# Linear attention and a residual MLP on one core: the beta2 product, the token mix, k^T v and VectorE's share rearranged, with a planner that looks ahead

## The chip, the cores and the metric

The kernel runs on one core of a Trainium2 chip. The metric is the device time in microseconds of one execution. TensorE (PE) multiplies matrices, VectorE (DVE), ScalarE (ACT) and GpSimd (POOL) do the elementwise work, SyncE (SP) issues most of the transfers.

## The reference

Eight batches, 8 heads of 64, 576 tokens; x has 512 features per token.

```python
kv  = einsum('bhsd,bhse->bhde', k, v)
out = einsum('bhsd,bhde->bhse', q, kv)
x   = out / sqrt(mean(out*out, -1) + 1e-6) * g_norm      # then heads side by side: [8, 576, 512]
a1  = alpha1 * x + beta1
u   = x + lam * einsum('ts,bsd->btd', w_tok, a1)
a2  = alpha2 * u + beta2
y   = u + lam * (maximum(a2 @ w_ch1, 0) @ w_ch2)         # w_ch1 512x2048, w_ch2 2048x512
```

## The kernel before

The whole problem is one program without loops on the device: Python calls `P.op(engine, cost, function, reads, writes)` for each group of instructions, and a planner (`Prog.plan`, `Prog.schedule`) orders them. It holds a cost for each op, makes a list schedule with them over all engines and the 8 banks of PSUM, works back from due times (`mark`) to new priorities for 8 rounds, keeps the best, shakes its priorities at random with a seed, and writes the last schedule down as each engine's fixed order. An engine takes the first op of its queue that is ready at the planned moment. On the chip each engine then follows its own list and waits on semaphores where an op needs another engine or a transfer. Before the first product of batch 0's first channel stage, whenever TensorE would have nothing ready in the plan, the planner puts in a product on zeros (`warm`, L1429).

A batch b goes through these stages:

- k, v and q are loaded in f32 (`load_kv`, `load_q`). Rows 0 to 511 of each head go to 128 partitions, 4 rows each, and the last 64 rows, the tail, to tensors of their own (kft, vft, qft). Batch 0 is loaded instead in two halves of four heads as 64 partitions by 9 rows (`load_first`, `nine`).
- `kv_groups`: k^T v per head in f32; two main groups (L691, 128 rows by 64 columns of the array) and one tail group (L701, 64x64). ScalarE and VectorE split the result into two bf16 parts and copy it to the other half of the partitions (L718, L723, L726). Batch 0 uses 64x64 quadrants (`kv_first`, L628).
- q is split in two bf16 parts (`split_q`, L582) and transposed: by TensorE for batch 1 (L605), by DMA for later batches; batch 0 is transposed in f32 (L649).
- `qkv_groups`: q times kv in pairs of token chunks (L782 with L401 on the held weights, tail L863; batch 0 L789), squares on ScalarE (L819), sums on VectorE (L821), square root on ScalarE, reciprocal, the normalised x (L840), then rt = x * (alpha1*lam*g) in bf16 on VectorE (L844; tail rtt, L892) and x*g in place on GpSimd (L848; tail L895).
- `tok_groups`: the token mix. W_tok^T lies in wt: slots 0 to 3 hold 128 rows each, slots 4 and 5 both hold the last 64 rows, at partitions 0 to 63 for even batches and 64 to 127 for odd ones, and each one also holds a row of W_tok's sums against a row beta1*lam in rtt; the rest is zeros. Each of four token chunks takes 5 passes of 512 columns (L920), and the tails of two batches are mixed together after the odd one (L942). Batch 0 has its own order in two halves of the features (`tok_first`, L972). VectorE adds the result to x (L927).
- u is scaled by alpha2 (L933) and transposed to a2t by DMA (L1037). Batches 0 and 1 are transposed by TensorE in four blocks of 128 features (L1007), and alpha2 and beta2 come in with the evacuation (L1017).
- `ch1_groups`: 16 groups of 4 products. Even batches take 512 tokens (L1056), odd ones 640 as 2 x 320 with the tails of both batches (L1075). relu goes to ht (L1046, L1045). From batch 2 on, beta2's part is a bias hb, which batch 0 gets from a one-column product behind each of its 64 products, on the weights already in the array (L401 out of b2c).
- `ch2_groups`: 16 products per token chunk (L1121), added to u by VectorE (L1131) and written out. w_ch2 is scaled by lam as it is cast to bf16 (L1357).

The q.kv groups of batch b+1 are given among the first-stage groups of batch b, the token mix behind them, and k^T v of batch b+2 among the second-stage groups. SP's queue is first in, first out: transfers that are given in a chain keep their order, and a transfer that waits holds those behind it. The order of all other ops is the planner's.

Of the kernel before, what the change touches and what calls it, by code (L numbers as in the profile page):

```python
# [15 lines left out]
NH = 8  # L16
S = 576
# [32 lines left out]
class Prog:  # L50
# [6 lines left out]
    def __init__(self, nc, stack):  # L57
# [9 lines left out]
        self.spare = 0.0  # L67

# [54 lines left out]
    def plan(self, due, rounds, seeds):  # L123
# [40 lines left out]
        def shake(pri, seed):  # L164
            rnd = random.Random(seed)
            return {o: pri[o] + (rnd.gauss(0.0, 2.0) if rnd.random() < 0.1 else 0.0)
                    for o in movable}
# [12 lines left out]
    def schedule(self):  # L180
# [67 lines left out]

        while left:
            progressed = False  # L250
            for e, q in queues.items():
                while q and free[e] <= t + 1e-9:
# [3 lines left out]
                    for o in cands:  # L256
                        if not ready(o, t):
                            continue
                        if takes_port(o, e) and port_free > t + 1e-9:
                            continue  # L260
                        if isinstance(o.eng, tuple) and better_elsewhere(o, e, t):
                            continue
                        pick = o
                        break
# [142 lines left out]
def bass_transnormer_attn__then__resmlp_affine_kernel(  # L407
# [15 lines left out]
    with ExitStack() as stack:  # L423
# [14 lines left out]
        b2c = sb("b2c", [128, 4], BF16)  # L438
        hb = sb("hb", [128, 16], F32)
        eps = sb("eps", [128, 1], F32)  # L440
        kf = sb("kf", [128, 2, NH, 4, DH], F32)
        vf = sb("vf", [128, 2, NH, 4, DH], F32)
        qf = sb("qf", [128, NH, 4, DH], F32)
        kft = sb("kft", [128, 2, 4, DH], F32)
        vft = sb("vft", [128, 2, 4, DH], F32)
# [18 lines left out]
        a2t = sb("a2t", [128, 4, TP], BF16)  # L464
# [9 lines left out]
        def nine(tile, a):  # L474
            return tile[:, a].rearrange("p h c d -> p (h c d)")[:, 0:1152].rearrange(
                "p (x c d) -> p x c d", x=2, c=9)

# [38 lines left out]

        HALVES = (slice(0, 4), slice(4, 8))
        ALL = (slice(0, 8),)

        def load_first(a):  # L520
            for key, src, tile in (("kf", k, kf), ("vf", v, vf)):
                P.op("SP", 0.6, lambda e, src=src, tile=tile: e.dma_start(
                    nine(tile, a).rearrange("p x c d -> p x (c d)"),
# [11 lines left out]
        def load_kv(b, go=()):  # L535
            j = (b + 1) % 2
            for tile, tl, src, n in ((kf, kft, k, "kf"), (vf, vft, v, "vf")):
                P.op("SP", 0.6, lambda e, tile=tile, src=src: e.dma_start(
                    tile[:, j].rearrange("p h c d -> p h (c d)"),
                    src[b, :, 0:512, :].rearrange("h (p c) d -> p h (c d)", c=4)),  # L540
                    r=go, w=[(n, j)], dma_us=3.4)
                for g in range(2):
                    P.op("SP", 0.5, lambda e, tl=tl, src=src, g=g: e.dma_start(
                        tl[64 * g:64 * g + 64, j],
                        src[b, 4 * g:4 * g + 4, 512:576, :].rearrange("h s d -> s h d")),
                        w=[(n + "t", j, g)], dma_us=0.4)
# [71 lines left out]

        def kv_first():

            def group(a):
                t = P.ptile(2)

                def f(e):
                    for c in range(9):
                        for x, y in ((0, 0), (0, 1), (1, 0), (1, 1)):
                            r = slice(64 * y, 64 * y + 64)
                            m = e.matmul(t.ap(slice(64 * x, 64 * x + 64))[:, y, 0:64],  # L628
                                         nine(kf, a)[r, x, c, :], nine(vf, a)[r, x, c, :],
                                         start=(c == 0), stop=(c == 8), skip_group_check=True)  # L630
                    return m
                P.op("PE", 1.22, f, r=[("kf", a), ("vf", a)], w=[t])
# [43 lines left out]

        def kv_groups(b):
            buf = (b + 1) % 2
# [6 lines left out]
            def main(a):  # L685
                ts.append(P.ptile(1))

                def f(e):
                    for c in range(4):
                        for h in range(4 * a, 4 * a + 4):  # L690
                            m = e.matmul(out(h), kf[:, buf, h, c, :], vf[:, buf, h, c, :],  # L691
# [5 lines left out]
            def tails():  # L697
                def f(e):
                    for h in (0, 4, 1, 5, 2, 6, 3, 7):
                        rows = slice(64 * (h // 4), 64 * (h // 4) + 64)  # L700
                        m = e.matmul(out(h), kft[rows, buf, h % 4, :], vft[rows, buf, h % 4, :],  # L701
                                     start=False, stop=True, skip_group_check=True)
                    return m
                P.op("PE", 0.4, f, r=[(n + "ft", buf, g) for n in "kv" for g in range(2)], w=ts)
# [40 lines left out]
        def rv(b, cs, lo=0, hi=DM):  # L745
            rows = rows_of(b, cs[0])
            if cs[0] == 4:
                return rtt[rows, b % 2, lo:hi]
# [14 lines left out]
        def qkv_groups(b):  # L763

            def group(cs, hs):
# [30 lines left out]
                if b == 0:  # L796
                    P.op("PE", 0.28 * nc_, f32, r=QT + KVD + [("kv32", h0 // 4, i)
# [37 lines left out]
                else:  # L835
# [7 lines left out]
                P.op(dve_pool(64 * m) if b == 0 else "DVE", dve_sb(64 * m),  # L843
                     lambda e: e.tensor_tensor(out=r_, in0=x, in1=eb, op=ALU.mult),  # L844
                     r=xk + ["e1"], w=[kk for c in cs for kk in rkeys(b, c, hs)], pri=-100, port=True)
                for i, c in enumerate(cs):
                    xc = x3[:, i] if nc_ > 1 else x3
                    P.op("POOL", pool_us(64 * nh), lambda e, xc=xc: e.tensor_tensor(  # L848
                        out=xc, in0=xc, in1=g_bc[rows, None, :].to_broadcast([nr, nh, DH]),
                        op=ALU.mult), r=xkeys(b, c, hs) + ["g"], w=xkeys(b, c, hs), pri=-50)  # L850
            def tail():
# [30 lines left out]
                for a in range(2):  # L882
# [9 lines left out]
                P.op("DVE", dve_sb(512), lambda e: e.tensor_tensor(  # L892
                    out=rv(b, (4,)), in0=x, in1=e1g_bc[rows, :], op=ALU.mult),
                    r=xk + ["e1"], w=rkeys(b, 4), pri=-100, port=True)
                P.op("POOL", pool_us(512), lambda e: e.tensor_tensor(  # L895
# [6 lines left out]
        def tok_w(b, sc, c):  # L902
            ws = sc if sc < 4 else 4 + b % 2
            return wt[:, ws, 128 * c:min(128 * c + 128, S)]
# [4 lines left out]
        def wtk(sc, b=0):  # L909
            return [("wtm", sc)] if sc < 4 else [("wts", 4 + b % 2, lo) for lo in (0, 512)]  # L910

        def tok_groups(b):
            def group(cs):
                n = len(cs)
                t = P.ptile(n)
                rows = rows_of(b, cs[0])
                for i, c in enumerate(cs):
# [544 lines left out]
```

## Time and profile before

| | us |
|---|---|
| median of 3 runs (lowest, highest) | 368.38 (367.87, 368.93) |
| the profiled execution | 368.05 |
| its span, first to last instruction | 366.2 |
| TensorE busy | 360.6 |
| VectorE busy | 198.4 |
| ScalarE busy | 159.2 |
| GpSimd busy | 81.7 |

The granted TensorE clock was 1.0 throughout. A busy TensorE counts each product from its start to the end of its result, 0.38 us for 512 columns, while the next starts 0.216 us after it; so costs on TensorE are read from starts, or from the chain, whose pieces follow each other without overlap. A row of the chain has its start, its length and its engine and line; a row of the timeline has start, length, engine, line, operation, output and inputs; a group of instructions has count, busy time, mean in ns, and the idle time before it with who ended it.

### The profile page before, as it was taken

What the parts mean: (1) busy time and instruction counts of PE and PEld (TensorE: products, weight loads), DVE (VectorE), ACT (ScalarE), POOL (GpSimd) and SP (SyncE); (2) the same over time, 40 slices, a digit from 0 to 9 for tenths busy, and PEclk for the clock granted to TensorE, in tenths of its full rate; (3) what the DMA queues carried; (4) which work ended last, traced back from release to release, by engine and by line L of the source; (5) the groups of instructions that cost most, each with busy time, mean ns of one, the idle gap of its engine ahead of it and who ended that gap; (6) DMA issues with size and microseconds to landing.
All of it is one profiled execution on the core that took longest, in us unless ns stands there. A gap on an engine that the chain in (4) does not pass through costs nothing.

```text
span 366.2 us, 7069 instructions
## 1 busy us (share of the span) xinstructions
PE 360.6 (98%) x3164; PEld 205.8 (56%) x2876; DVE 198.4 (54%) x313; ACT 159.2 (43%) x268; POOL 81.7 (22%) x71
## 2 busy tenths in 40 slices
PE   7999999999999999999999999999999999999996
PEld 3787445467754554457654554457654554457644
DVE  4287699773973197735764176915933165720021
ACT  2464974237830298107650188107630186007600
POOL 4064602700450007100530006400620006200000
PEclk9999999999999999999999999999999999999999
DMA  8999999999777897439904499233404110420012
GB/s 257 319 290 319 384 382 273 265 250 249 211 141 158 246 259 178 101 94 309 230 18 115 138 304 177 50 110 85 90 7 108 59 30 0 59 100 30 0 57 88
DMA packets 92423, 59.87 MB, mean 163 GB/s; under 512 B 59549, under 2 KB 82341, under 8 KB 92264
## 3 DMA queue, kind: packets, MB, share of 16 engines
q1 hardware_dynamic: 92368, 59.41, 62.5%
q8 instruction: 24, 0.39, 0.5%
q14 instruction: 7, 0.06, 0.0%
q10 hardware_dynamic: 24, 0.01, 0.0%
HBM read 38.56 MB, written 9.44 MB: 131 GB/s over the span
## 4 chain that ended last, share of the span: by engine, by line
PE 97%; DMA 2%; SPq 0%; DVE 0%; issue 0%
PE ps L1121 34%; PE ps L1075 19%; PE ps L1056 16%; PE ps L920 8%; PE ps L691 4%; DMA qf<-in_q_dram 2%; PE ps L401 2%; PE ps L782 2%; PE ps L789 1%; PE ps L942 1%; PE ps L972 1%; PE ps L1007 1%; PE ps L1429 1%; PE ps L649 1%; PE ps L1102 1%; PE ps L701 1%
## 5 line engine op out<-in xcount | busy, mean ns | idle before, releaser
L1121 PE MATMUL ps<-w,ht 128*128 128x512 bf16 x560 | 126.0, 379 | 0.0
L848 POOL TENSOR_TENSOR xm<-xm,g_bc 128x512 f32<-128x512 f32 (+1 forms) x36 | 47.4, 1316 | 186.6 <-DVE rt L844 184.7
L1121 PEld LDWEIGHTS ps<-w,ht 128*128 128x128 bf16 x560 | 53.1, 98 | 63.0 <-issue 1.2
L1045 ACT ACTIVATE ht<-ps,hb 128x512 bf16<-128x512 f32 (+1 forms) x96 | 70.5, 739 | 40.5 <-PE ps L1075 32.8
L1075 PE MATMUL ps<-a2t,w 128*128 128x320 bf16 x512 | 71.9, 299 | 0.0
L1075 PEld LDWEIGHTS ps<-a2t,w 128*128 128x128 bf16 x512 | 49.3, 98 | 20.2 <-ACT ht L1045 0.3
L1056 PE MATMUL ps<-a2t,w 128*128 128x512 bf16 x256 | 59.7, 379 | 0.0
L1131 DVE TENSOR_TENSOR xm<-ps,xm 128x512 f32<-128x512 f32 x31 | 21.4, 689 | 50.4 <-PE ps L1121 50.3
L718 ACT ACTIVATE kvd<-ps 64x128 bf16<-64x128 f32 x28 | 7.6, 271 | 78.5 <-PE ps L701 78.1
L1056 PEld LDWEIGHTS ps<-a2t,w 128*128 128x128 bf16 x256 | 24.3, 97 | 29.6 <-issue 1.2
L821 DVE TENSOR_REDUCE small<-sq 128x16 f32<-128x1024 f32 (+2 forms) x20 | 20.5, 1028 | 22.9 <-ACT sq L819 22.9
L920 PE MATMUL ps<-rt,wt 128*128 128x512 bf16 x112 | 28.8, 379 | 0.0
L501 ACT ACTIVATE qs<-qf 128x1024 bf16<-128x1024 f32 (+1 forms) x15 | 14.2, 964 | 26.7 <-DMA qf<-in_q_dram 26.1
L927 DVE TENSOR_TENSOR xm<-ps,xm 128x1024 f32<-128x1024 f32 x14 | 17.1, 1222 | 14.5 <-PE ps L920 14.5
L1046 ACT ACTIVATE ht<-ps 128x512 bf16<-128x512 f32 (+1 forms) x32 | 20.6, 650 | 6.8 <-PE ps L1075 3.3
L819 ACT ACTIVATE sq<-ps 128x1024 f32<-128x1024 f32 (+2 forms) x20 | 17.4, 873 | 7.3 <-PE ps L789 4.3
L840 DVE TENSOR_TENSOR xm<-ps,small 128x1024 f32<-128x1024 f32 (+1 forms) x18 | 19.8, 1103 | 0.4
L723 DVE TENSOR_TENSOR kvd<-ps,kvd 64x128 bf16<-64x128 f32 x28 | 8.1, 288 | 20.5 <-ACT kvd L718 20.0
L844 DVE TENSOR_TENSOR rt<-xm,e1g_bc 128x1024 bf16<-128x1024 f32 (+1 forms) x17 | 19.0, 1125 | 0.1
L582 DVE TENSOR_TENSOR qs<-qf,qs 128x1024 bf16<-128x1024 f32 x12 | 15.3, 1284 | 6.8 <-ACT qs L501 6.8
L920 PEld LDWEIGHTS ps<-rt,wt 128*128 128x128 bf16 x112 | 10.9, 98 | 12.9 <-issue 0.4
L691 PEld LDWEIGHTS ps<-vf,kf 128*64 128x64 f32 x448 | 14.2, 138 | 5.0 <-issue 5.0
(119 smaller groups left out, 334.2 us busy)
## 6 DMA issues: line engine op xcount, KB each, us to landing
out_dram<-xm SPq DMA_DIRECT2D x31, 256.0 KB, 2.5
kf<-in_k_dram SPq DMA_DIRECT2D x7, 1024.0 KB, 10.3
vf<-in_v_dram SPq DMA_DIRECT2D x7, 1024.0 KB, 8.0
qf<-in_q_dram SPq DMA_DIRECT2D x7, 1024.0 KB, 8.0
stg<-in_moe_w_ch_dram SPq DMA_DIRECT2D x3, 1024.0 KB, 13.8
kf<-in_moe_w_ch_dram SPq DMA_DIRECT2D x2, 1024.0 KB, 14.6
kf<-in_k_dram SPq DMA_DIRECT2D x2, 576.0 KB, 5.2
vf<-in_v_dram SPq DMA_DIRECT2D x2, 576.0 KB, 6.3
```

Of the source, the lines that this page charges most:

```text
L691: m = e.matmul(out(h), kf[:, buf, h, c, :], vf[:, buf, h, c, :], start=(c == 0 and h < 4 * a + 2), stop=False, skip_group_check=True)
L821: P.op("DVE", dve_us(64 * m), lambda e: e.tensor_reduce(out=smv, in_=sqv.rearrange("p (h d) -> p h d", h=m), axis=AX.X, op=ALU.add), r=[(" ...
L840: P.op("DVE", dve_us(64 * m), lambda e: e.tensor_tensor(out=x3, in0=split(raw()), in1=inv, op=ALU.mult), r=[t, ("sm", sms)], w=xk, pri=-200)
L844: lambda e: e.tensor_tensor(out=r_, in0=x, in1=eb, op=ALU.mult),
L848: P.op("POOL", pool_us(64 * nh), lambda e, xc=xc: e.tensor_tensor(out=xc, in0=xc, in1=g_bc[rows, None, :].to_broadcast([nr, nh, DH]), op=A ...
L920: m = e.matmul(t.ap()[:, i, :], tok_w(b, sc, c), rsrc(b, sc), start=(sc == 0), stop=(sc == 4))
L1045: o = P.op("ACT", act_us(n) + 0.09, lambda e: e.activation(dst, src(), ACT.Relu, bias=hb[:, fj:fj + 1]) if b > 1 else e.activation(dst, sr ...
L1046: dst, src(), ACT.Relu, bias=hb[:, fj:fj + 1]) if b > 1 else e.activation(
L1056: m = e.matmul(t.flat(), w, a2t[:, dj, 0:512], start=(dj == 0), stop=(dj == 3))
L1075: m = e.matmul(t.ap()[:, i, 0:320], w1[:, dj, 128 * fj:128 * fj + 128], a2t[:, dj, 320 * i:320 * i + 320], start=(dj == 0), stop=(dj == 3))
L1121: m = e.matmul(t.flat(), ht[:, fj, 128 * c:128 * c + 128], w2[:, fj, :], start=(fj == 0), stop=(fj == 15))
L1131: P.op("DVE", dve_us(512), lambda e: e.tensor_tensor(out=x, in0=t.flat(), in1=x, op=ALU.add), r=[t] + keys, w=keys)
```

## The change

- beta2: its four columns stand in a2t as column 640 (a2t is 16 wider). Batch 1's second half takes 321 columns instead of 320, and the last one is copied to hb group by group. The one-column products of batch 0 and b2c are gone.
- First channel stage of batch 0: the first four groups are cut in two. `front` takes the products on the first half of a2^T's features, `back` those on the second half into the same bank; each can be planned by itself.
- `kv_groups` for batches 2 to 7 is `kv_nine`: batch 0's layout and its 64x64 quadrants, two groups. k and v then come in one transfer each, with no tails.
- Token mix for batches 2 to 7: 4 full passes per chunk, then one pair of 64-row products for two chunks, from slot 4 (rows 0 to 63) and slot 5 (rows 64 to 127). The sums row and the beta1 row drop out there; rt gets the beta1 term by an addition on VectorE (lam_bc is overwritten with beta1*lam once w_ch2 has been scaled), by way of the scratch sq, and rtt is copied to the other half of the partitions.
- W_tok's tail is evacuated once, and slot 5 is a VectorE copy of slot 4.
- x*g goes to VectorE for batches 2 to 7.
- The planner: an engine of ScalarE, VectorE and GpSimd leaves an op alone if a more urgent one will be ready within half its cost (`sooner`); other shares and sizes of the shaking, five seeds instead of one; some costs corrected. alpha1, lam and the other parameter rows are fetched in a fixed order.

```diff
+        def sooner(o, e, t):
+            cost = o.cost[e] if isinstance(o.cost, dict) else o.cost
+            until = t + self.look * cost
...
+                    if t + 1e-9 < at <= until:
+                        return True
...
+                        if e in ("ACT", "DVE", "POOL") and sooner(o, e, t):
                             continue
...
-        a2t = sb("a2t", [128, 4, TP], BF16)
+        a2t = sb("a2t", [128, 4, TP + 16], BF16)
...
+        def kv_product(b, a):
+            j = a if b == 0 else (b + 1) % 2
+            t = P.ptile(2)
+            def f(e):
+                for c in range(9):
+                    for x, y in ((0, 0), (0, 1), (1, 0), (1, 1)):
+                        r = slice(64 * y, 64 * y + 64)
+                        m = e.matmul(t.ap(slice(64 * x, 64 * x + 64))[:, y, 0:64],
+                                     nine(kf, b, a)[r, x, c, :], nine(vf, b, a)[r, x, c, :],
+                                     start=(c == 0), stop=(c == 8), skip_group_check=True)
...
+                    P.op("DVE", dve_sb(64 * m), lambda e: e.tensor_tensor(
+                        out=sv, in0=x, in1=eb, op=ALU.mult), r=xk + ["e1"], w=[("sq", sqs)],
+                        pri=-100, port=True)
+                    P.op("DVE", dve_sb(64 * m), lambda e: e.tensor_tensor(
+                        out=r_, in0=sv, in1=eb2, op=ALU.add), r=[("sq", sqs), "e2"], w=rk,
+                        pri=-100, port=True)
...
+                    P.op("DVE", 0.3, lambda e: e.tensor_copy(
+                        out=rtt[64:128, b % 2, :], in_=rv(b, (4,))),
...
+                    def g(e):
+                        for i, c in enumerate(cs):
+                            r = slice(64 * i, 64 * i + 64)
+                            m = e.matmul(t.ap()[:, i, :], wt[r, 4 + i, 128 * c:128 * c + 128],
+                                         rtt[r, b % 2, :], start=False, stop=True)
...
-                        if b == 0:
-                            m = P.matmul_held(hbt.flat()[:, fj:fj + 1], w, b2c[:, dj:dj + 1],
-                                              dj == 0, dj == 3)
...
+            def front(fj):
+                held[fj] = t = P.ptile(1)
+                def f(e):
+                    for dj in range(2):
+                        m = e.matmul(t.flat(), w1[:, dj, 128 * fj:128 * fj + 128],
+                                     a2t[:, dj, 0:512], start=(dj == 0), stop=False)
...
+                            n = 321 if (b, i) == (1, 1) else 320
...
-        P.plan(due, 8, (15,))
+        P.plan(due, 8, (53, 59, 68, 82, 104))
```

285 lines of the change are left out of this document (190 added, 95 removed).

## The prediction

> **What bounds the kernel now.** I read the page's head first (share of each engine, the chain that ended last), then who waited on TensorE, then the chain in order of time.
>
> ```profile
> PE 360.6 (98%) x3164; PEld 205.8 (56%) x2876; DVE 198.4 (54%) x313; ACT 159.2 (43%) x268; POOL 81.7 (22%) x71
> PE 97%; DMA 2%; SPq 0%; DVE 0%; issue 0%
> PE ps L1429 <- DVE a2b L1226: 1.9, 1, 1.9
> PE ps L649 <- DMA qf<-in_q_dram: 0.3, 1, 0.3
> ```
>
> TensorE is busy for 360.6 of 366.2 us, it makes 97% of the chain, and the two waits in the whole list lie before 8.8 us. From there to the last product no other engine is waited for. So the time is the sum of what stands in TensorE's queue. An edit is worth what it takes out of that queue, less any wait that it opens; VectorE at 54% and GpSimd at 22% cost nothing so far. Some of the queue is not work: L1429 is the filler, a product on zeros that the planner puts in where it expects TensorE to have nothing until the first product of batch 0's first channel stage.
>
> ```profile
> 7.84 0.60 PE L1429 MATMUL ps<-a2b 128*128 128x512 bf16 x2
> 8.76 1.97 PE ps L649 x32
> 11.15 0.32 PE ps L1429
> 11.47 1.05 PE ps L1198 x2
> 12.52 1.67 PE ps L789 x12
> 15.40 1.09 PE ps L789 x8
> 16.49 1.90 PE ps L649 x32
> 18.65 1.62 PE ps L1429 x7
> 36.69 1.94 PE ps L1429 x9
> 38.63 0.21 PE ps L1056
> ```
>
> Each row is start, length, what. Between 7.84 and 38.63 us there is 0.92 us up to the landing of q (two fillers and the wait of 0.3) and then 0.32 + 1.62 + 1.94 = 3.88 us of filler.
>
> **Part 1: beta2 as a 321st column.** Before, each of the 64 products of batch 0's first channel stage is followed by a one-column product on the same weights.
>
> ```profile
> L401 PE MATMUL ps<-b2c,w 128*128 128x1 bf16 x64 | 10.5, 164 | 0.0
> 45.08 0.38 PE L1056 MATMUL ps<-a2t,w 128*128 128x512 bf16 x1
> 49.90 0.38 PE L1056 MATMUL ps<-a2t,w 128*128 128x512 bf16 x1
> 71.56 2.16 PE ps L920 x10
> 169.89 1.09 PE ps L1075 x8
> ```
>
> From the L1056 at 45.08 to that at 49.90 there are 20 products: 4.82 / 20 = 0.241 us each. A bare product of 512 columns takes 2.16 / 10 = 0.216. So the one-column product costs 0.025 us, and 64 of them 1.6 us, all on the path. In their place 64 products of batch 1 get one column more: 320 columns take 1.09 / 8 = 0.136 us, one column 0.0004, all 0.03 us. The 16 copies of one column into hb ride on ScalarE and VectorE during batch 1's first channel stage, whose groups last 1.09 us each. Net -1.57 us.
>
> **Part 2: k^T v of batches 2 to 7 in two groups of 64x64 quadrants, instead of two main groups and a tail.**
>
> ```profile
> 14.19 1.21 PE ps L628 x72
> 120.04 1.08 PE ps L691 x32
> 125.87 0.39 PE ps L701 x16
> 149.92 0.38 PE L920 MATMUL ps<-rtt,wt 128*128 128x512 bf16 x1
> 150.22 1.05 PE L942 MATMUL ps<-rt,wt 128*64 128x512 bf16 x8
> 151.11 0.38 PE L942 MATMUL ps<-rtt,wt 128*64 128x512 bf16 x2
> 151.43 0.39 PE L1121 MATMUL ps<-w,ht 128*128 128x512 bf16 x1
> ```
>
> L628 is the new form, used today for batch 0. The other rows give the price of a change of tile shape: from the last full product at 149.92 to the first 128x64 product 0.30 us pass instead of 0.216, and from the last pair at 151.11 to the full product 0.32. So each change of shape costs 0.09 to 0.1 us. The 1.08, 0.39 and 1.21 already hold the way out; the way in is added. Before: 2 x 1.08 + 0.39 + 3 x 0.09 = 2.82 us a batch. After: 2 x (1.21 + 0.09) = 2.60. Six batches: -1.3 us.
>
> **Part 3: token mix in 18 passes, batches 2 to 7.** The fifth pass over s has only 64 real rows. Two chunks now share it, one in array rows 0 to 63 (wt slot 4), one in rows 64 to 127 (slot 5, a copy), into two banks. That takes out 2 passes a batch, 2 x 0.216 = 0.43 us, 2.6 us in all. But the order of the changed kernel has each pair by itself behind 8 full products, so the shape changes twice per pair, and 4 times a batch: 4 x 0.095 = 0.38. In odd batches the tail mix also ends in a 64x64 shape, but its way in is then from a pair and not from a full product, so the count stays 4. Net 0.05 us a batch, -0.3 us in all. Do the two halves overlap? L628's 72 products of 64 columns take 16.8 ns each and L691's 32, on 128 rows, 34 ns: halves of the rows under the same columns do run side by side, into different banks, and I take that. If they don't, each pair costs 0.216 more.
> The Trainium skill, "TensorEngine Tiling (Array Packing)", has two rules here. Its table under Theoretical Speedup promises up to 2x for a small contraction, which alone would make this part -2.6 us. Its Key Properties say that a change of tiling mode drains the array, and give no price; the rows at 149.92 to 151.43 bear that out, and by them little of the gain is left.
>
> **Part 4: the start.** Three things move in TensorE's order. alpha1 is fetched second instead of sixth, so the broadcast of alpha1 (the L1198 at 11.47, 1.05 us) stands in the hole before q lands.
>
> ```profile
> 4.69 1.38 DVE L1190 TENSOR_TENSOR rtt<-xm 1x512 bf16<-1x512 f32 x2 [2.89 <-DMA xm<-in_moe_beta_dram]
> 7.69 0.49 SPq L1222 DMA_DIRECT2D ht<-in_moe_w_tok_dram  x1
> ht<-in_moe_w_tok_dram SPq DMA_DIRECT2D x1, 144.0 KB, 11.6
> 28.16 2.15 SPq L1340 DMA_DIRECT2D kf<-in_moe_w_ch_dram  x1
> kf<-in_moe_w_ch_dram SPq DMA_DIRECT2D x2, 1024.0 KB, 14.6
> 45.89 0.68 DVE L502 CAST w<-kf 128x1024 bf16<-128x1024 f32 x1
> 39.58 0.47 PE ps L605 x8
> ```
>
> The row that is fetched second today, beta1, was there at 4.69. alpha1 in its slot, with two one-row products on VectorE behind it, is ready before 7.84. The broadcast ends at 7.84 + 1.05 = 8.89, just after q: 0.92 us gained. Fillers behind it are 14 instead of 17, 14 x 0.216 = 3.02 us against 3.88: 0.86 gained. Does a wait open? Adding the rows in the new order, 8.89 + 1.97 (L649) + 0.42 (its tail and alpha2/beta2) + 0.86 + 2.76 (L789) + 1.90 + 1.21 (L649, L628) + 0.27 + 0.65 gives 18.9 us at the first transpose of W_tok, whose last rows land at 7.69 + 11.6 = 19.3: a wait of 0.4. Together -1.4; for small waits in the tighter stretch I take -1.3, with ends -1.8 (all five stretches as the fillers have it) and -0.3.
> The products on half of a2^T (four groups of two, and four more that finish them) take no TensorE time of their own; they stand where the nine fillers stood, and the work behind them comes sooner: the first at 38.6 - 1.4 + 0.5 = 37.7 us, since one q^T group (L605, 0.47) is now ahead of it. What is late next is VectorE. In its new order the cast of w_ch1's third block comes ahead of the copies of kv and the evacuation of q^T of batch 1. That block lands at 28.16 + 14.6 = 42.8; today VectorE takes it at 45.89 with no wait, in the new order it gets there at about 40.5 and stands for 2 us with some 4.5 us of work queued behind. TensorE needs the block at its ninth group (30 products and 20 transposes on: 37.7 + 6.5 + 1.2 = 45.4; cast by 44.8) and the banks held by kv and q^T one or two groups later (about 47, freed at 47 to 48). I take +0.5 us, with ends 0 and +1.5.
>
> **Part 5: VectorE takes x*g and the beta1 term in batches 2 to 7.** No TensorE time, but more work ahead of the token mix. The tightest batch today:
>
> ```profile
> 223.77 1.23 DVE L844 TENSOR_TENSOR rt<-xm,e1g_bc 128x1024 bf16<-128x1024 f32 x1
> 225.03 0.69 DVE L892 TENSOR_TENSOR rtt<-xtl,e1g_bc 64x512 bf16<-64x512 f32 x1
> 226.91 4.32 PE ps L920 x20
> L726 DVE COPY kvd<-kvd 64x256 bf16<-64x256 bf16 x28 | 6.1, 222 | 0.6
> ```
>
> rt is done at 225.0, 1.9 us ahead of the mix; the fifth pass needs rtt at 226.91 + 0.86 = 227.77, 2.05 us ahead. New work before rt: two additions of the beta1 term and one x*g of 1.2 us each, 3.6 us. Before rtt another addition (0.7) and the copy to the other half (0.22 for half the columns, so some 0.35): 4.7 us. The new order pays for this: 16 products of the second channel stage stand before the mix instead of 4 (12 x 0.216 = 2.6 us later), the first q.kv products stand 4 products of the first stage sooner (0.86), and rtt is used after 8 products rather than 4 (0.86). Left: 1.9 + 2.6 + 0.86 - 3.6 = 1.8 us for rt, and 2.05 + 2.6 + 0.86 + 0.86 - 4.7 = 1.7 for rtt. So cost 0. If the cover is gone, every microsecond past 1.7 is paid six times. GpSimd's work of those batches is gone, which takes a neighbour off VectorE's port and not off the path. W_tok's second tail copy and its memset were off the path too.
>
> **Sum.** -1.57 - 1.3 - 0.3 - 1.3 + 0.5 = -4.0 us. The profiled execution took 368.05 us (span 366.2), 0.33 under the median 368.38. So 364.1 beside it, and 364.4 beside the median. A change of 0.3%, 1.1 us, is about what a measurement can tell.
>
> **The rivals.**
> - *The halves do not overlap* (chance 0.07). The pairs then cost 12 x 0.216 = 2.6 us more: 367.0, still just faster. For it: no row has 64x128 tiles with 512 columns. Against it: the quadrants of L628.
> - *The start gives nothing and VectorE's early cast holds TensorE* (0.11): part 4 at -0.3 + 1.5: -2.0 in all, 366.4. For it: a block that lands under full DMA load can come later than 42.8. This is also the case in which the early half products do not do what they say. They start early and the rest waits.
> - *The slower side: VectorE's longer chain opens a wait before each token mix* (0.12). It decides from 1.7 us of slip in each batch; TensorE's gain of 4.0 us is gone when the wait is over 0.67 us in each of six batches, that is from a slip of 2.4. A slip of 3 us gives 6 x 1.3 = 7.8, so 372.2. For it: a square root on ScalarE sits between VectorE's reductions and queues behind the relus, and the waits pass on to a2^T by DMA. Against it: every row of the chain is counted at its full time, and 1.7 us is left.
> - *Changes of shape are free for row halves* (0.03), as the table cited in part 3 would have it: part 3 is then -2.6 instead of -0.3, 362.1. For it: the rows at 150.22 and 151.43 are of column tiles. Against it: the way into 64x64 quadrants costs as much.
> - *As the sum says* (0.67): 363.0 to 366.0 with parts 2 and 3 between -1.1 and -2.0 and part 4 between its ends.
>
> **How the numbers follow.** The likeliest is the sum, 364.4. The range goes from 362.9 (start at -1.8, no stall, parts 2 and 3 at -2.0) to 368.0, which holds the first two rivals and the mild end of the third; what is left out is the rest of the third and surprises, under 0.2. Faster than 367.3: the sum and most of the first two rivals, 0.83. Within 0.3%: 0.06. Slower: 0.11, nearly all of the third.
>
> **What would show it.** Right: TensorE still has no releaser but the first two and one on W_tok; its busy time falls by about 4; no one-column products; L1056's heir at 0.216; the first product on a2^T at about 37.7 with one q^T group done before it; pairs of the mix that start 4 to 7 ns apart with 0.3 us on each side. Wrong: rows of TensorE waiting for VectorE's rt or rtt every 40 us; the two halves 0.216 us apart; a gap of over 1.5 us between 40 and 50 us.

## The result, and the profile after

The changed kernel takes 364.71 us (median of 4 runs, 363.64 to 365.61); the kernel before took 368.12 beside it (4 runs, 367.66 to 368.93). The ratio is 0.9904 (95% interval 0.9875 to 0.9932). The forecast was 364.4, with 362.9 to 368.0 as its range. The profiled execution took 365.61, with a span of 363.6 us.

First the page of the changed kernel: TensorE's busy time (360.6 before), the queue that brings instructions, and the shares of the chain that ended last.

```profile
PE 357.7 (98%) x3479; PEld 203.9 (56%) x3255; DVE 240.8 (66%) x366; ACT 160.2 (44%) x277; POOL 26.6 (7%) x34
...
q8 instruction: 26, 0.43, 0.5%
...
PE 98%; DVE 0%; issue 0%
```

TensorE is 2.9 us less busy, 1.4 us at half rate included (below), and still is the whole chain. Next what TensorE waited for, by the waits of the changed kernel (waiting group, releaser, total us, times, longest):

```profile
PE ps L1572 <- DVE a2b L1368: 1.9, 1, 1.9
PE ps L1169 <- issue: 0.8, 1, 0.8
```

The first is the start of the program. The forecast's wait on W_tok is not there: its last rows land at 17.6 us (18.8 in the repeat below) and not at 19.3, and TensorE comes for them at 20.3 (19.5). The second is new, and nobody forecast it: TensorE stands in the middle of first channel products and waits for no semaphore ("issue"). Most of the experiments went into it.

Then the start, from the chain in order of time (start, length, what):

```profile
1.87 5.73 PE ps L1572 x13
7.59 0.52 PE ps L1340 x2
8.11 1.21 PE ps L666 x72
9.32 1.05 PE ps L1340 x2
10.37 1.90 PE ps L693 x32
...
19.75 0.75 PE ps L1572 x3
20.50 0.47 PE ps L1402 x4
...
38.44 1.29 PE ps L1184 x6
39.73 0.45 PE ps L644 x8
40.18 0.86 PE ps L1196 x4
...
45.23 3.45 PE ps L1169 x16
```

Read it so: thirteen fillers (L1572) take 5.73 us, 0.44 each, and not 0.216: TensorE ran at half its rate until about 7.8 us (the two L1340 behind the fillers still take 0.52 us, 0.36 in the repeat below). In the profile of before the first seven fillers take 0.427 us each too, and the full rate comes at 4.9 us. The clock in the profile's rows does not tell of it: it reads 1.00 from 4 to 8 us here, and the 1.0 given for the kernel before holds only behind its start. k^T v (L666) begins at 8.11, 1.4 us later than in the profile of before. The broadcast of alpha1 (the second L1340) and q^T (L693) follow with no hole, W_tok (L1402) is not waited for, and the first product on half of a2^T (L1184) comes at 38.44; the q^T group ahead of it is the L644 at 37.55 of the same chain. L1169, the heir of L1056, takes 3.45 / 16 = 0.216 us a product. Nothing stands still between 40 and 50 us.

Last the token mix, from the timeline of TensorE (start, length, group):

```profile
103.93 0.39 PE L1029 MATMUL ps<-rtt,wt 64*128 64x512 bf16 x2
104.25 1.90 PE L1020 MATMUL ps<-rt,wt 128*128 128x512 bf16 x8
106.08 0.39 PE L1029 MATMUL ps<-rtt,wt 64*128 64x512 bf16 x2
106.41 0.39 PE L1260 MATMUL ps<-w,ht 128*128 128x512 bf16 x1
```

A pair occupies 106.41 - 106.08 = 0.33 us for both its products (0.32 at 103.93): the halves overlap (their starts lie 3 to 4 ns apart in the trace), and the way out of the shape costs 0.10. The way in costs the same: the last full product starts 0.31 us ahead of the pair, and not 0.216.

To see which batch gave what, the table below takes from each trace the time from the first product of one stage to that of the next (us; worked out from the records of the profiled executions, no view prints it; "ch1(b)" is the first channel product of batch b that sets its stage).

```
                   before  after  repeat  20 passes  pairs  old k^Tv  one-col  q late
start to k^T v(0)    6.63   8.04    7.18     7.54     7.78     6.55     6.42    7.03
to ch1(1)           76.24  72.54   72.38    72.37    72.38    74.78    75.44   72.38
ch1(1) to ch1(2)    44.20  44.00   44.00    44.01    43.79    45.73    44.19   44.00
ch1(2) to ch1(3)    38.47  38.23   38.23    38.22    38.02    38.26    39.06   38.23
ch1(3) to ch1(4)    44.19  43.94   43.94    44.38    43.72    44.42    43.94   43.94
ch1(4) to ch1(5)    38.47  39.21   39.18    38.22    38.94    38.26    38.23   40.89
ch1(5) to ch1(6)    44.19  43.94   43.94    43.94    43.73    44.42    43.94   43.94
ch1(6) to ch1(7)    35.59  35.60   35.60    35.59    35.39    35.39    35.60   35.60
ch1(7) to the end   38.24  38.09   38.09    38.09    38.09    38.23    38.08    38.09
```

From before to after it is 1.4 us lost ahead of k^T v, 3.7 won up to batch 1, 0.20 to 0.25 won in each of five steps, nothing in the sixth, 0.15 at the end, and 0.74 lost from ch1(4) to ch1(5) where 0.24 should have been won: 0.98 us have gone there.

### The profile page after: what moved, and what is told of

It reads as the page before. It is cut to its first block, busy times and chain, and to the rows that moved or that the text cites. A ratio compares the mean times of both kernels' runs of the same rounds, so it can differ in the third digit from the quotient of the medians.

```text
span 363.6 us, 7716 instructions
## 1 busy us (share of the span) xinstructions
PE 357.7 (98%) x3479; PEld 203.9 (56%) x3255; DVE 240.8 (66%) x366; ACT 160.2 (44%) x277; POOL 26.6 (7%) x34
## 4 chain that ended last, share of the span: by engine, by line
PE 98%; DVE 0%; issue 0%
PE ps L1260 34%; PE ps L1211 19%; PE ps L1169 14%; PE ps L1020 7%; PE ps L666 5%; PE ps L1572 2%; PE ps L851 2%; PE ps L428 2%; PE ps L1053 1%; PE ps L858 1%; PE ps L1083 1%; PE ps L1118 1%; PE ps L693 1%; PE ps L1029 1%; PE ps L1241 1%; PE ps L951 1%
## 5 line engine op out<-in xcount | busy, mean ns | idle before, releaser
L1260 PE MATMUL ps<-w,ht 128*128 128x512 bf16 x560 | 125.8, 379 | 0.0
L1260 PEld LDWEIGHTS ps<-w,ht 128*128 128x128 bf16 x560 | 53.3, 98 | 62.9 <-issue 1.4
L1211 PE MATMUL ps<-a2t,w 128*128 128x320 bf16 (+1 forms) x512 | 72.4, 299 | 0.0
L1211 PEld LDWEIGHTS ps<-a2t,w 128*128 128x128 bf16 x512 | 49.4, 98 | 20.5
L1169 PE MATMUL ps<-a2t,w 128*128 128x512 bf16 x240 | 55.3, 379 | 0.8 <-issue 0.8
L728 ACT ACTIVATE kvd<-ps 64x128 bf16<-64x128 f32 x24 | 6.5, 271 | 92.3 <-PE ps L666 92.2
L1169 PEld LDWEIGHTS ps<-a2t,w 128*128 128x128 bf16 x240 | 22.4, 98 | 26.4 <-issue 1.3
L1020 PE MATMUL ps<-rt,wt 128*128 128x512 bf16 x112 | 26.9, 380 | 0.0
L733 DVE TENSOR_TENSOR kvd<-ps,kvd 64x128 bf16<-64x128 f32 x24 | 6.9, 289 | 18.6 <-ACT kvd L728 18.3
L666 PEld LDWEIGHTS ps<-vf,kf 64*64 64x64 f32 x1008 | 16.0, 135 | 4.6 <-issue 4.6
L666 PE MATMUL ps<-vf,kf 64*64 64x64 f32 x1008 | 17.8, 221 | 0.0
L1270 DVE TENSOR_TENSOR xtl<-ps,xtl 128x512 f32<-128x512 f32 x4 | 2.8, 692 | 20.2 <-PE ps L1260 20.1
L1041 DVE TENSOR_TENSOR a2b<-xm,a_bc 128x512 bf16<-128x512 f32 x24 | 15.5, 687 | 0.4
```

The source lines that it names most:

```text
L666: m = e.matmul(t.ap(slice(64 * x, 64 * x + 64))[:, y, 0:64], nine(kf, b, a)[r, x, c, :], nine(vf, b, a)[r, x, c, :], start=(c == 0), stop= ...
L1020: m = e.matmul(t.ap()[:, i, :], tok_w(sc, c), rsrc(b, sc), start=(sc == 0), stop=(sc == 4))
L1169: m = e.matmul(t.flat(), w, a2t[:, dj, 0:512], start=(dj == 0), stop=(dj == 3))
L1211: m = e.matmul(t.ap()[:, i, 0:n], w1[:, dj, 128 * fj:128 * fj + 128], a2t[:, dj, 320 * i:320 * i + n], start=(dj == 0), stop=(dj == 3))
L1260: m = e.matmul(t.flat(), ht[:, fj, 128 * c:128 * c + 128], w2[:, fj, :], start=(fj == 0), stop=(fj == 15))
L1270: P.op("DVE", dve_us(512), lambda e: e.tensor_tensor(out=x, in0=t.flat(), in1=x, op=ALU.add), r=[t] + keys, w=keys)
```

## The experiments

All twelve runs compare with the kernel before on their own chip (medians 368.40 to 368.55).

**The change again.** Same code.

> The changed kernel once more, for a second profile and a tighter time. Theory (TensorE's queue is the time): 364 to 365.5 us; no releaser on TensorE from the first transposes of q on. Two things of the first profile are open. Its TensorE ran the 13 leading fillers at 0.427 us each and started k^T v 1.4 us later than in the profile of before: if that is the moment at which the clock comes up, it will differ here by up to 1.5 us, and the time with it. And it had one gap of 1.0 us at 207 us, in which TensorE waited for nothing that the profile shows: if it is a fetch of instructions behind transfers it can be absent or elsewhere; if it belongs to the order of the work it comes back at the same product.

Measured: 364.56 us (364.07 to 365.02, 5 runs), ratio 0.9892 (0.9878 to 0.9907). The fillers left the half rate at 6.1 us instead of 7.2, so k^T v began at 7.18. The hole stood behind the same product of the order, 1.16 us from start to start. So the late full rate varies from run to run; the hole belongs to the kernel.

**Token mix in 20 passes.**

```diff
-        MIX = 2
+        MIX = 8
```

> The token mix of batches 2 to 7 goes back to 20 passes, with the sums row and the beta1 row (no addition of the beta1 term on VectorE, no copy of rtt); all else as in the changed kernel. Theory (a change of tile shape costs 0.1 us, so 18 passes save only 0.03 to 0.05 us a batch): +0.2 to +0.3 us against the changed kernel, within the noise. Rival (18 passes save 2 x 0.216 us a batch, the drain is hidden): +2.6 us. Rival (VectorE's longer chain costs TensorE something): faster than the changed kernel by over 0.5 us.

Measured: 364.24 us (363.75 to 364.44, 4 runs), ratio 0.9883 (0.9868 to 0.9898). In the table its steps are those of 18 passes to 0.01 us, but for one step 0.44 longer (a wait for VectorE) and one without the hole. So part 3 is worth nothing: four changes of shape eat the two passes.

**Both pairs of a batch together.**

```diff
-                    P.op("PE", 0.28, g, r=wtk(4) + ["wt5"] + rkeys(b, 4), w=[t])
+                    mixed.append((cs, t))
+                    if len(mixed) < 2:
+                        return
...
+                    P.op("PE", 0.62, g, r=wtk(4) + ["wt5"] + rkeys(b, 4), w=[y for _, y in mixed])
```

> The two row-half pairs of a batch's token mix stand together, behind all 16 full passes, instead of one behind each 8. Nothing is added or taken out but one way in and one way out of the 64x128 shape per batch. Theory (0.1 us for each change of shape, in both ways): 6 x 0.2 = 1.2 us faster than the changed kernel, about 363.5. Rival (the drain is hidden, or the pair costs its time anyway): no change. Rival (the later end of the first half of the mix holds VectorE and the transposes of a2): slower.

Measured: 363.58 us (362.40 to 363.86, 5 runs), ratio 0.9858 (0.9840 to 0.9875), the best of all kernels here. The steps are 0.20 to 0.22 us shorter: two changes of shape less, so 0.10 for each, as the forecast had priced them.

**Pairs together and k^T v in one piece.** On top of that edit, all 144 quadrant products of a batch as one group.

```diff
-            for a in range(2):
-                yield lambda a=a: group(a)
+            yield both
```

> As the kernel with the pairs together, and k^T v of batches 2 to 7 in one piece: both groups of quadrants behind each other into one pair of banks, so 64x64 is entered once a batch and not twice. Theory: another 5 x 0.19 = 0.95 us (in the first of the six batches they stood together already), about 2.1 us under the changed kernel in all: 362.5. Rival (changes of shape are not what it costs): 364.7 as the changed kernel. Rival (2.4 us of k^T v in one piece come too late or hold banks): TensorE shows waits for kv or for banks, and it is slower than the kernel with the pairs alone.

Measured: 369.37 us (366.37 to 370.62, 12 runs), ratio 1.0020 (1.0002 to 1.0038). A miss by 7 us. By the waits of this kernel:

```profile
PE ps L1199 <- issue: 2.8, 1, 2.8
...
PE ps L1241 <- ACT a2t L1157: 0.9, 1, 0.9
PE ps L1036 <- DVE xm L1065: 0.7, 1, 0.7
PE ps L1241 <- DVE hb L534: 0.3, 1, 0.3
PE ps L1241 <- DMA a2t<-a2b: 0.3, 1, 0.3
```

The hole has grown to 2.96 us, and the planner's new order opened four waits. The idea itself held where neither stands in the way: from ch1(2) to ch1(3) it takes 37.74 us (38.02 with the pairs alone), from ch1(3) to ch1(4) 43.46 (43.72), two changes of shape less a batch. The profiled run (366.37) is the fastest of the twelve and had the full clock (mean 1.0); the other eleven showed a mean clock of 0.989 to 0.995. That made the hole the question. These rows of the changed kernel bear on it: TensorE around the hole, SyncE's queue, and the transfer queues from 206.1 to 207.4 us.

```profile
206.75 1.03 PE L1169 MATMUL ps<-a2t,w 128*128 128x512 bf16 x4
208.59 0.60 PE L1169 MATMUL ps<-a2t,w 128*128 128x512 bf16 x2 [0.81 <-issue]
```

```profile
199.73 0.43 SPq L537 DMA_DIRECT2D qf<-in_q_dram  x1
200.21 0.71 SPq L544 DMA_DIRECT2D qft<-in_q_dram  x1
...
206.00 0.39 SPq L572 DMA_DIRECT2D kf<-in_k_dram  x1
206.44 1.18 SPq L572 DMA_DIRECT2D vf<-in_v_dram  x1
```

```profile
q1 hardware_dynamic: 127, 0.13, 46.5%
q8 instruction: 1, 0.02, 4.8%
```

The columns of the last view are packets, MB and share of the transfer queues. The queue named "instruction" moves 26 packets of 16,384 bytes in the whole execution, one per 261 of TensorE's 6797 records. The trace dates the one in this window at 206.22 to 207.21, and TensorE goes on 1.37 us after it has landed. The q load of batch 6 was issued at 199.73, and the queues were busy until 206. The theory: TensorE ran out of instructions, because the next piece of them stood behind the q load. The place is a likely one: the quadrants of k^T v are 144 products with 144 weight loads a batch, and the last 268 records ahead of the hole passed in 5.4 us (202.0 to 207.4) where the mean is 14. Four runs tried it.

**Thirteen fillers as twenty-six.** 26 more instructions ahead of everything, in the same time; no other order changes.

```diff
+            if len(sent) <= 13:
+                e.matmul(t.flat()[:, 0:256], wz[:, 0:128], wz[:, 0:256], start=True, stop=True)
+                return e.matmul(t.flat()[:, 256:512], wz[:, 0:128], wz[:, 256:512],
+                                start=True, stop=True)
```

> The changed kernel's order, but each of the 13 leading filler products of 512 columns goes out as two of 256: the same time, 13 more products with their weight loads, 26 more TensorE instructions ahead of everything else. Asked: is the hole of 1.2 us (pitch 1.16 to 1.19 us) between two first channel products at 206.4 to 207.4 us the end of TensorE's loaded instructions? Theory A (instruction load): TensorE's instructions come in pieces of 16,384 bytes about every 257 of its records; the piece that the hole waits for stood behind the q load of batch 6 (1 MB, issued at 199.7) until 206.2 and landed at 207.2; TensorE ran out at its record 4288. With 26 records more ahead it runs out 26 records earlier, 13 products of 0.216 us, while the piece lands as before: the hole grows by 2.8 us to about 4.0 us, it begins at about 203.6 (start of the run as in the repeat), and the time is about 367.4 us (366.8 to 368). Theory B (something at this place in the work, a hidden wait of the products): the hole stays 1.2 us at the same product, 364.6 us. Theory C (chance of the transfers): the hole comes or goes anywhere, 363.5 to 364.6.

Measured: median 364.67 us (363.68 to 367.78, 10 runs), ratio 0.9914 (0.9891 to 0.9937); the profiled run took 367.31. TensorE in that run:

```profile
203.81 0.81 PE L666 MATMUL ps<-vf,kf 64*64 64x64 f32 x40
206.65 0.38 PE L666 MATMUL ps<-vf,kf 64*64 64x64 f32 x4 [2.04 <-issue]
207.36 1.06 PE L1260 MATMUL ps<-w,ht 128*128 128x512 bf16 x2 [0.33 <-issue]
```

In the change the hole came behind all of k^T v, four second channel products (L1260) and four first ones (L1169). Here it comes ahead of all these and of the last four of k^T v: with their weight loads 24 instructions earlier in the order, where 26 were added. It lasts 2.25 us, and a little behind it six products of 512 columns take 0.427 us instead of 0.216 and a seventh 0.367: the clock had fallen (a mean of 0.50 from 207 to 210 us). Hole and slow products make the step from ch1(3) to ch1(5) 4.0 us longer than without a hole, 3.0 over the repeat. The forecast had 2.8 for the hole alone; 1.4 of the 3.0 are the slow products, which it did not have, so the hole grew by 1.6. And the median stayed: of ten runs three (367.1 to 367.8, the profiled one among them) show a mean clock of 0.994 to 0.995, and the other seven (363.7 to 365.3) are about as fast as the change. So the place is set by the count of instructions; the size seems to be set by when the piece comes, and to vary from run to run.

**Six fillers fewer.** 12 instructions fewer, fillers 2 to 7 left out, all else the same.

```diff
+            if 1 < len(sent) <= 7:
+                return None
```

> The changed kernel's order without 6 of the 13 leading fillers (12 TensorE instructions fewer). Two readings from one run. Hole at 206 to 207 us: theory A (instruction load) has TensorE run out 12 records later, 6 products of 0.216 us = 1.3 us, where the hole was 0.95 to 1.2 us over a product: hole gone or under 0.2 us; theory B: hole stays. Start: the fillers took 0.427 us each until 6.1 to 7.2 us, so k^T v began at 7.2 to 8.0 instead of the 6.6 of the kernel before. Without 6 of them (2.6 us at the slow rate) k^T v begins when its k and v rows have landed, about 6.2 us, 1.0 to 1.8 us earlier; rival: the full clock comes later without them and the first products take twice as long, which gives back up to 1.2 us. Sum by A: 364.6 - 1.0 for the hole - 0.2 to 1.4 for the start = 362.2 to 363.4, likeliest 362.6. By B with no gain at the start: 364.6.

Measured: 366.31 us (363.51 to 368.13, 10 runs), ratio 0.9938 (0.9915 to 0.9961). The hole, from TensorE's timeline:

```profile
210.27 1.03 PE L1169 MATMUL ps<-a2t,w 128*128 128x512 bf16 x4
211.13 0.19 PE L851 MATMUL ps<-kvd,qt 128*128 128x64 bf16 x1
211.16 0.19 PE L428 MATMUL ps<-kvd,qt 128*128 128x64 bf16 x1
212.02 0.20 PE L851 MATMUL ps<-kvd,qt 128*128 128x64 bf16 x1 [0.67 <-issue]
```

It moved down, past the rest of the eight first channel products and into the q^T·(k^T v) products: the 12 instructions. It didn't close (0.83 us), and one more of 0.73 us opened at 81.95. The forecast (362.2 to 363.4) was missed, and the start is the larger lesson. From the chain of the profiled run, which is the slowest of the ten (368.13):

```profile
1.24 4.88 DMA vf<-in_v_dram
...
6.16 2.20 PE ps L666 x72
8.36 2.00 PE ps L1340 x2
10.36 3.61 PE ps L693 x32
```

k^T v begins at 6.16, when v has landed, 1.0 us sooner than in the repeat; but TensorE started nothing from 5.23 to 6.16, the full rate came at about 14.2 us instead of 6.1, and at W_tok's transposes the kernel is 2.7 us behind. The fillers pay for themselves; that the pause put the full rate off is argued from this one profile. The Trainium skill, "TensorE: Matmul & The Clock Gate", Part 1, says that the clock rises after one busy window of some 3.4 us that runs freely and isn't tied to the kernel's start. The traces agree: in the thirteen others of this case the fillers begin at 1.86 or 1.87 us, and the full rate comes anywhere from 4.5 to 7.8 us.

**The q load of batch 6 behind the k and v loads of batch 7.** SyncE's queue alone changes.

```diff
+        late = [loads["q", 6], loads["qt", 6]]
+        for o in late:
+            seq.remove(o)
+        i = seq.index(loads["vf", 7]) + 1
+        seq[i:i] = late
```

> The changed kernel with one edit on SyncE's queue: the q load of batch 6 (1 MB and its 128 KB tail, issued at 199.7 us in the changed kernel) goes behind the k and v loads of batch 7 (issued at 206 us); every other order is the same. Theory A (TensorE's instruction piece stands behind the q load): the piece is asked for about 257 records ahead, near 202 us, now finds the transfer queues free, lands by about 204 and TensorE passes its record 4288 without a hole: 364.6 less 0.95 = 363.6 us (363.2 to 364.0), and the runs lie closer together. q of batch 6 is first read at 216.4 us, so nothing waits for it if it lands by 217. Theory B (the hole belongs to the products or to the k and v loads): the hole stays, 364.6. Theory C: the next piece (needed near record 4545 at 221 us) is now the late one, behind three loads: a hole moves to 221 us, 364.0 to 365.5.

Measured: 365.80 us (365.40 to 366.12, 5 runs), ratio 0.9923 (0.9906 to 0.9940). The piece of instructions starts at 202.26 and lands at 203.2, and the hole at 206 us is gone: theory A holds. The run with 20 passes says the same without an edit to the loads: its order issues the q load at 195.03, the piece starts at 202.98, and there is no hole. The time rose all the same: a wait opened where no theory had one. From SyncE's timeline, TensorE's waits and ScalarE's waits:

```profile
204.83 0.39 SPq L574 DMA_DIRECT2D kf<-in_k_dram  x1
205.26 0.51 SPq L574 DMA_DIRECT2D vf<-in_v_dram  x1
205.81 0.51 SPq L537 DMA_DIRECT2D qf<-in_q_dram  x1
206.36 4.66 SPq L544 DMA_DIRECT2D qft<-in_q_dram  x1
```

```profile
PE ps L1174 <- ACT ht L1163: 2.5, 1, 2.5
```

```profile
ACT qs L533 <- DMA qft<-in_q_dram: 3.6, 1, 3.6
```

The small tail of q lands 11.6 us after its issue, near 218 us. ScalarE's split of it, which ran at 216.4 in the change, stands in ScalarE's queue and holds the relus behind it, and TensorE lacks a bank at 216.3: 2.65 us. To move the large load alone and leave the tail where it was would be the next thing; it was not tried.

**Pairs together and q late.** Both edits.

> Both 64-row pairs of a batch together (as in the run with pairs together, 363.6 us) and the q load of batch 6 behind the k and v loads of batch 7. Theory A: the two gains add, 363.6 - 0.95 = 362.6 us (362.2 to 363.1), with no hole at 206 us. Theory B: the hole stays and the time is 363.6.

Measured: 365.00 us (364.67 to 365.28, 4 runs), ratio 0.9904 (0.9887 to 0.9921): the hole is gone here too (piece at 201.98), the same wait stands at 216.1 (2.1 us), and the pairs bring their 0.2 a batch.

**k^T v as before.**

```diff
-            if b > 1:
-                yield from kv_nine(b)
-                return
```

> k^T v of batches 2 to 7 back in the form of the kernel before (64 products 128x64 and 16 of 64x64 a batch, loads in 512 and 64 rows), the rest of the change as it is; the planner orders anew. Theory: the quadrant form gives 0.22 us a batch (2.82 against 2.60), 1.3 us over six batches, and costs 64 products more a batch with their weight loads, 128 TensorE instructions, which run a piece of 257 instructions dry in some 2.4 us; without them the hole near 206 us goes. Sum 364.6 + 1.3 - 0.95 = 364.9 us (364.4 to 365.6). Rival: the hole has nothing to do with the number of instructions and stays where it was: 365.9. Second rival: k^T v lies off the path: 363.6 to 364.6.

Measured: 368.08 us (367.57 to 370.15, 12 runs), ratio 0.9996 (0.9981 to 1.0011). The new order brought waits that have nothing to do with k^T v:

```profile
PE ps L1251 <- DVE w L1484: 2.6, 1, 2.6
...
PE ps L1202 <- DVE kvd L783: 0.8, 1, 0.8
```

They stand at 54.3 and 83.9 us. The steps that they don't touch tell the price: from ch1(2) to ch1(4) it takes 82.68 us, with the quadrants 82.17, 0.255 a batch less. The kernel before takes 82.66 there, so k^T v is the whole gain of these steps, and nothing is left for the token mix. And no hole of TensorE's near 206, with 23 pieces instead of 26.

**beta2 back in one-column products.**

```diff
+                        if b == 0:
+                            m = one(fj, dj)
...
-                            n = 321 if (b, i) == (1, 1) else 320
+                            n = 320
```

> beta2's part back in one-column products beside the first channel products of batch 0 (64 of them, with the weights held), 320 columns in batch 1; the first groups on half of a2^T keep two partial columns that are added later. Theory: 64 products of one column at 0.027 us each less the 321st column (64 x 0.002): 1.6 us more, 364.6 + 1.6 = 366.2 us (365.6 to 366.8) with the hole as it is. By the instruction theory the 64 instructions more move the dry place 64 records up, into the k^T v products, where it begins 2.5 us earlier: in the executions in which the piece is late as well the hole is 2 us or more, and the clock falls behind it: up to 369. Rival: the one-column products hide behind others and cost nothing: 364.6.

Measured: 366.93 us (366.16 to 367.56, 6 runs), ratio 0.9957 (0.9941 to 0.9974). From k^T v(0) to ch1(1) it takes 3.06 us more than in the repeat, 1.24 of them at a wait of its new order (xm, at 71.5 us). Of the other 1.82 the products account for 1.6: batch 0's first channel products start 0.241 us apart here as in the kernel before, 0.025 more than bare ones, 64 times. The last 0.2 belong to the rest of the new order. The dry place moved here as well: the piece came at 201.88 and there is no hole at 206, but one of 0.84 at 127.9.

**No products on half of a2^T.**

```diff
-        FRONT = 4
+        FRONT = 0
```

> No first channel product on half of a2^T: batch 0's groups all wait for the whole a2^T, the rest of the change as it is. Theory: the four groups ahead fill what else are fillers; six more fillers of 0.216 us or a wait of the same length stand before the first channel product, so the first whole group of batch 0 comes 1.3 us later (half groups 8 x 0.43 us less work ahead of it, of which the order takes 2.2 us for other work) and the time is 364.6 + 1.3 = 365.9 (365.2 to 366.4). Rival: the planner finds other work (q^T groups) for the place and it costs nothing: 364.6. The hole at 206 us may be there or not, 1 us either way, to be read in the trace and taken out of the comparison.

Measured: 367.58 us (366.70 to 370.70, 12 runs), ratio 0.9991 (0.9971 to 1.0010). The first channel products begin at 39.00 with five fillers ahead, and from k^T v(0) to ch1(1) it takes 2.80 us more than in the repeat. One microsecond of that is a wait of ch1(1) for a2^T on VectorE, so the four groups are worth some 1.8, or 2.8 with what hangs on them. The hole has 1.63 us here.

**x\*g on GpSimd.**

```diff
-                P.op("POOL" if b < 2 else "DVE", pool_us(n) if b < 2 else dve_sb(n),
+                P.op("POOL" if b < 8 else "DVE", pool_us(n) if b < 8 else dve_sb(n),
```

> x*g back on GpSimd in all batches as in the kernel before, the rest of the change as it is. Theory: off the path on either engine (each stayed 1.7 us ahead of its reader in the kernel before), so 364.6 plus or minus the hole at 206 us (0 to 1.2). Rival: VectorE alone with the beta1 add saves a wait per batch: 366 and TensorE with waits on xm of 0.2 us or more a batch. Second rival: VectorE was loaded by it, and without it the time falls by over 0.5 us with no change in the hole.

Measured: 365.92 us (364.56 to 367.94, 6 runs), ratio 0.9929 (0.9912 to 0.9947). The waits of TensorE:

```profile
PE ps L1211 <- DVE xm L909: 1.9, 1, 1.9
...
PE ps L1029 <- DVE rtt L992: 0.9, 3, 0.3
```

These are of the slowest of the six runs (367.94). Not free after all: in this order three pairs wait 0.3 us each for rtt, and once VectorE itself stood 2.9 us for a store of xm. Whether the latter belongs to GpSimd or to the new order stays open.

The holes, taken together (us; from the traces):

```
                       piece lands   TensorE goes on   after
the change                 207.21         208.58        1.37
the repeat                 206.21         207.53        1.32
pairs together             205.90         207.26        1.35
k^T v in one piece         209.07         210.31        1.24
26 fillers                 205.30         206.65        1.35
six fillers fewer           81.47          82.74        1.27
six fillers fewer          210.65         212.02        1.37
no half products           208.52         209.85        1.33
x*g on GpSimd              208.85         210.23        1.38
one-column products        127.38         128.78        1.41
```

## Why the prediction was right, and where only by luck

The sign, the size and the cause (TensorE's own work falls by 4 us) are right. By its steps:

- **Part 1** (-1.57): -1.6 by the one-column run, where the products start 0.241 us apart again. Right.
- **Part 2** (-1.3): six times 0.255, -1.5. Right; the two forms lie 0.255 us a batch apart where the forecast had 2.82 against 2.60.
- **Part 3** (-0.3): 0.0. The mechanism is right, the term was too large. Each change of shape costs 0.10 and not 0.095, and four of them are the whole gain of 0.43. The rule of the Trainium skill that the forecast cites, that a change of tiling mode drains the array ("TensorEngine Tiling (Array Packing)", Key Properties), is borne out by the pairs run: two changes less, 0.20 to 0.22 less.
- **Part 4** (-1.3 and +0.5): the work from k^T v on gained more, and the stall of +0.5 did not come. Up to ch1(1) the change is 2.29 us ahead; less 1.6 for part 1 and 0.25 for the first batch of part 2 that is -0.44, in the repeat -1.46. Without the fillers' delay (1.41 and 0.55) both come to -1.85 to -2.0, a little beyond the end of -1.8 that the forecast gave the start. This is what is left over and holds the planner's whole new order. The step that failed is "VectorE takes the block late and TensorE stands": no row of TensorE waits there. And the start itself was taken from one profile in which the full rate came early; at 7.8 instead of 4.9 us it takes back 1.4.
- **Part 5** (0): no wait on rt or rtt in the change, so the cover held.
- **Not in the forecast:** the hole (+0.98) and a shorter end (-0.15). The change adds 64 products and as many weight loads a batch, and the forecast counted their time only, not the instructions that must be brought.

Sum: -1.6 - 1.43 (part 2 as it stands in the steps) - 1.85 + 1.41 + 0.98 - 0.15 = -2.64, against -2.63 between the two spans (366.21 and 363.58). The forecast had -4.0. Parts 1, 2, 4 and the end were better than forecast by 1.4 together; part 3 and the hole were worse by 1.3, and these cancel: that the sum came out so near is luck, as nothing ties the one to the other. What is left, 1.4, is the late full rate of the one execution that was profiled (365.61); the repeat had 0.55 of it (364.56), and the median of 364.71 lies 0.3 from the forecast.

None of the rivals came. The halves overlap, the chain of VectorE opens no wait, and changes of shape aren't free.

What stays open: no run had the old planner with the new work, so what of part 4 comes from the planner's rule and its seeds was not measured apart, and the experiments that change the work were ordered anew, which can add waits of their own. That the piece waits behind the q load is shown by moving the load; that its size differs from run to run of one program is argued from the times alone, and why it should isn't known. That the lower mean clock of eleven runs with k^T v in one piece comes from longer holes is argued from the run with 26 fillers, where one profile shows hole and slow products together; those eleven have no profile.

## What to carry over

Price an edit that splits products in instructions too, not only in array time: TensorE went through 268 records in 5.4 us here, and a 1 MB load issued just before made it wait for the next piece. When a profile shows TensorE idle with "issue" as its releaser, look for the last packet of the instruction queue: if TensorE goes on some 1.3 us after it, the cure is in the queue of transfers. And small tiles pay only in runs: put products of one odd shape side by side before counting the passes saved.

## What the runs showed that was not expected

- TensorE's instructions come in packets of 16,384 bytes, one per about 260 records, and a late one stops it; it goes on 1.24 to 1.41 us after the packet has landed (ten cases). The Trainium skill, "Runtime: NRT & Kernel Launch", Instruction fetch mechanics, has blocks of 16 KiB and 256 instructions and calls the cost of crossing one "mostly hidden". The trace agrees for 25 of the 26 of the changed kernel; the other costs 0.98 us, and 2.96 with k^T v in one piece.
- The rate of the first fillers: half until 4.9 us in the profile of before, until 5.4 to 7.8 in those of the changed order. With six fillers fewer and nothing started from 5.23 to 6.16 us, the full rate came at about 14.2.
- A stretch of 2.9 us with only four small products was followed by six products at half rate and a seventh in part; one of 3.0 us with none (k^T v in one piece) was not.
